# An attention and state-space kernel: the state-space half computed by another route

## The chip, the cores and the metric

The kernel runs on one core of a Trainium2 chip. The metric is the device time of one execution in microseconds (us); six runs of the kernel before are shown. The engines are TensorE (PE; PEld is its weight load), VectorE (DVE), ScalarE (ACT), GpSimd (POOL) and SyncE (SP); SP, ACT and POOL also issue DMAs, each on a queue of its own.

## The reference

Two independent results stand side by side in the output, [1, 2048, 896]: 448 columns of a linear attention, and 448 of a long convolution whose kernel K comes from a diagonal state-space model.

```python
def _A_ref(x, wqkv, w_phi, wo):            # x [1, 2048, 448], 16 heads of 28
    q, k, v = split(x @ wqkv)
    phi = lambda t: concat(softmax(t @ w_phi), softmax(-(t @ w_phi)))
    kv = einsum("bhsf,bhsd->bhfd", phi(k), v);  z = sum_s(phi(k))
    return (phi(q) @ kv / (phi(q) @ z + 1e-6)) @ wo

def _B_ref(u, A_re, A_im, B_re, B_im, C_re, C_im, log_dt, Dskip):   # u [1, 2048, 448], states 448 x 256
    dt = exp(log_dt)[:, None]
    logdA, dB = dt * (A_re + 1j * A_im), dt * (B_re + 1j * B_im)
    l = arange(2048).astype(bf16)          # rounded: only 641 different values
    K = einsum("dn,dnl,dn->dl", C, exp(logdA[:, :, None] * l), dB).real
    y = irfft(rfft(pad(u)) * rfft(pad(K)))[:2048]                   # length 4096
    return y + u * Dskip
```

The positions l are rounded to bfloat16 in the reference: 0 to 256 are exact, above that they come in steps of 2, 4 and 8.

## The kernel before

The program is written in a framework that makes the waits and orders the instructions of each engine itself, from the order of the program and from which of them it reckons to be ready. A pool that takes over the SBUF of released pools waits until these are no longer used.

`hedgehog_attention` comes first: loads of x and the weights, q, k and v (ps_qk at L195, written ahead of ps_v at L210), the exponentials and their sums, the feature sums, the result (ps_out, L423) and its stores (osb). `ssm_conv` follows in four steps.

`ssm_coefficients` loads the six parameter tables transposed (tin_Are and so on) and makes the products with dt. `ssm_build_K` makes K as a sum over states of A^(64 h) times A^l. For each half of the states (nch) and each of 8 chunks of 14 x 4 channels it doubles two tables of powers: U (UR, UI; 32 high powers times C and B) and W (WR, WI; 65 low powers), with `_cmul` (L494 to L499), six VectorE tensor_tensors a step:

```python
nc.vector.tensor_tensor(out=t1, in0=ar, in1=brb, op=ALU.mult)
nc.vector.tensor_tensor(out=t2, in0=ai, in1=bib, op=ALU.mult)
nc.vector.tensor_tensor(out=out_r, in0=t1, in1=t2, op=ALU.subtract)
...
```

For each channel two small matmuls (L609, L611) sum over 128 states: weights U of 32 columns, moved W of 65, four channels side by side in the four column groups of the array. The results go to Ts, and from there to a table kd in DRAM (L622).

`ssm_fft_conv` builds its Fourier tables on the chip, then transforms u and K in two stages each (psA at L792, then xps at L826) with a round trip through DRAM between them (SD_u, SD_k), multiplies the two spectra (L874 to L879), and transforms back in two stages with another round trip (ZD; zps, ops). The skip term u * Dskip joins in the last matmuls, and ob carries the result to the output (L936, L942).

Of the kernel before, what the change touches and what calls it, by code (L numbers as in the profile page):

```python
# [10 lines left out]
BF16 = mybir.dt.bfloat16  # L11
# [7 lines left out]
D_MODEL = 448  # L19
# [12 lines left out]


MAGIC_ROUND = 12582912.0


def round_f32(nc, out_ap, in_ap):
    nc.vector.tensor_scalar(out_ap, in_ap, MAGIC_ROUND, -MAGIC_ROUND, op0=ALU.add, op1=ALU.add)


def floor_div_const(nc, pool, out_ap, in_ap, shape, P, tag):
    t = pool.tile(shape, F32, name="fdt", tag=tag)
    nc.vector.tensor_scalar(t, in_ap, 1.0 / float(P), 0.5 / float(P) - 0.5, op0=ALU.mult, op1=ALU.add)
    round_f32(nc, out_ap, t)
# [26 lines left out]
def kernel(  # L71
# [371 lines left out]
DEBUG_TENSORS = {}  # L443
DEBUG_MODE = False
PI = float(np.pi)

N_LO = 65
N_HI = 32
N_ARG = 2 * N_LO


def ssm_coefficients(tc, B_A_re, B_A_im, B_B_re, B_B_im, B_C_re, B_C_im, B_log_dt, base_pool):
    nc = tc.nc
    A_nd = base_pool.tile([128, 2, D_MODEL], F32, name="A_nd")
    TH_nd = base_pool.tile([128, 2, D_MODEL], F32, name="TH_nd")
    CBR_nd = base_pool.tile([128, 2, D_MODEL], F32, name="CBR_nd")
    CBIN_nd = base_pool.tile([128, 2, D_MODEL], F32, name="CBIN_nd")
    with tc.tile_pool(name="coefT_in", bufs=1) as tin, \
         tc.tile_pool(name="coefT_w", bufs=1, side="right") as w:
        ldt_b = tin.tile([128, D_MODEL], BF16, name="ldt_b")  # L460
        nc.sync.dma_start(out=ldt_b[:, :], in_=bass.AP(tensor=B_log_dt.tensor, offset=B_log_dt.offset,
                                                         ap=[[0, 128], [1, D_MODEL]]))
        dt_b = tin.tile([128, D_MODEL], F32, name="dt_b32")
        nc.scalar.activation(dt_b[:, :], ldt_b[:, :], ACT.Exp)
        dtb_b = tin.tile([128, D_MODEL], BF16, name="dtb_b")
        nc.vector.tensor_copy(dtb_b[:, :], dt_b[:, :])
        for nch in range(2):
            T = {}
            for q_i, (nm, src) in enumerate((("Are", B_A_re), ("Aim", B_A_im), ("Bre", B_B_re),
                                              ("Bim", B_B_im), ("Cre", B_C_re), ("Cim", B_C_im))):  # L470
                t = tin.tile([128, D_MODEL], BF16, name=f"tin_{nm}", tag=f"tin_{nm}")
                eng = nc.sync if q_i % 2 == 0 else nc.scalar
                eng.dma_start(out=t[:, :], in_=src[:, nch * 128:(nch + 1) * 128], transpose=True)
                T[nm] = t
            nc.vector.tensor_tensor(out=A_nd[:, nch, :], in0=T["Are"][:, :], in1=dtb_b[:, :], op=ALU.mult)
            nc.vector.tensor_tensor(out=TH_nd[:, nch, :], in0=T["Aim"][:, :], in1=dtb_b[:, :], op=ALU.mult)
            dBr = w.tile([128, D_MODEL], F32, name="tdBr", tag="tdBr")
            dBi = w.tile([128, D_MODEL], F32, name="tdBi", tag="tdBi")
# [23 lines left out]
def ssm_build_K(tc, kd, A_nd, TH_nd, CBR_nd, CBIN_nd, base_pool, dbg=False):  # L502
# [4 lines left out]
    with tc.tile_pool(name="k_const", bufs=1) as cpool, \  # L507
# [6 lines left out]
        for nch in range(2):  # L514
# [26 lines left out]
            for k in (2, 4, 8, 16):  # L541
                P[k] = square(*P[k // 2], f"h{k}")
# [456 lines left out]
```

## Time and profile before

| | |
|---|---|
| median of 6 runs | 1189.57 us (1187.42 to 1190.99) |
| the profiled execution | 1189.7 us |
| its span, first to last instruction | 1187.6 us |
| TensorE / VectorE / ScalarE / GpSimd busy | 444.7 / 729.3 / 150.2 / 256.0 us |
| mean granted clock of TensorE | 0.595 of full speed |
| moved by DMA | 61.10 MB |

A busy time is the sum of an engine's instructions; shares over the whole span mix stages with different limits. PEclk is the granted clock of TensorE, 1.00 being 2.4 GHz and 0.50 being 1.2. The profile gives each instruction's start and length; instructions of one engine can overlap a little.

### The profile page before, as it was taken

The numbers are of one execution on the slowest core, as the hardware profiler recorded it, in microseconds if no ns is written. First come the engines' busy times: TensorE is split into PE (matmuls) and PEld (weight loads), VectorE is DVE, ScalarE is ACT, GpSimd is POOL, SyncE is SP. The second block draws the span as 40 slices with busy tenths as digits, with TensorE's granted clock in tenths as the row PEclk, the third lists the DMA queues.
The fourth block names the chain that finished last, engine by engine and source line by source line (L and its number), as shares of the span: only waits on it lengthen the run. The fifth ranks groups of instructions, "written<-read, shape, count | busy, mean of one in ns | idle before, by whom it ended". The sixth has DMA issues, their size and how long they took to land.

```text
span 1187.6 us, 10352 instructions
## 1 busy us (share of the span) xinstructions
PE 444.7 (37%) x3499; PEld 166.7 (14%) x3499; DVE 729.3 (61%) x1655; ACT 150.2 (13%) x200; POOL 256.0 (22%) x442
## 2 busy tenths in 40 slices
PE   1986544856800111121102112112334444163298
PEld 0221100511200111121102112110111111010021
DVE  1339337525339999999999999949423224832500
ACT  0113320001213000000000000003212222031000
POOL 1000010000008544584773753001000000010000
PEclk9995555666955565556556555555556556555555
DMA  5000000000120000000000000050575656056611
GB/s 126 1 0 1 0 0 0 4 2 0 61 52 1 1 1 1 1 1 1 1 0 2 1 1 1 2 84 10 155 213 175 148 144 248 15 130 164 248 31 31
DMA packets 60508, 61.10 MB, mean 51 GB/s; under 512 B 28904, under 2 KB 57120, under 8 KB 60224
## 3 DMA queue, kind: packets, MB, share of 16 engines
q1 hardware_dynamic: 30042, 31.22, 9.7%
q10 hardware_dynamic: 28782, 22.81, 7.1%
q0 software_dynamic: 1632, 6.42, 1.6%
q8 instruction: 27, 0.44, 0.2%
q14 instruction: 25, 0.20, 0.1%
HBM read 29.35 MB, written 27.61 MB: 48 GB/s over the span
## 4 chain that ended last, share of the span: by engine, by line
DVE 47%; PE 24%; DMA 18%; ACT 4%; issue 3%; POOL 1%; ACTq 1%; SPq 0%; DVEq 0%; POOLq 0%
DVE rt L494 5%; DVE rt L495 4%; DVE rt L498 4%; DVE rt L497 4%; PE ps_qk L195 3%; DVE WR L496 3%; DVE WI L499 3%; PE ops L930 2%; PE ops L928 2%; DMA xin<-kd 2%; PE num_ps L396 2%; DMA s2k<-SD_u 2%; PE psA L792 2%; DMA s2k<-SD_k 2%; PE ps_pq L268 2%
## 5 line engine op out<-in xcount | busy, mean ns | idle before, releaser
L609 PE MATMUL kps<-WR,UR 128*32 128x65 bf16 x896 | 64.8, 308 | 386.3 <-DVE WR L496 308.1
L609 PEld LDWEIGHTS <-UR 128*32 128x32 bf16 x896 | 49.0, 141 | 390.7 <-DVE WR L496 241.8
L792 PE MATMUL psA<-xin,FA 32*128 32x448 bf16 x128 | 51.8, 564 | 96.2 <-DVE stgA L805 34.1
L805 DVE CAST stgA<-psA 128x1792 bf16<-128x1792 f32 x16 | 32.4, 2022 | 69.1 <-PE psA L792 58.9
L611 PE MATMUL kps<-WI,UI 128*32 128x65 bf16 x896 | 60.0, 307 | 10.6 <-POOL qc32i L554 4.5
L611 PEld LDWEIGHTS <-UI 128*32 128x32 bf16 x896 | 48.1, 142 | 14.4 <-DVE WI L499 14.4
L195 PE MATMUL ps_qk<-xT,Wqkv 128*128 128x512 bf16 (+3 forms) x128 | 38.2, 411 | 28.5 <-DMA xT<-in_A_x_dram 25.6
L928 PE MATMUL ops<-ZA,IA 128*32 128x448 bf16 x64 | 35.4, 556 | 33.9 <-DMA ZA<-ZD 33.9
L499 DVE TENSOR_TENSOR WI<-rt,rt 128x448 bf16<-128x448 bf16 (+3 forms) x96 | 45.4, 473 | 0.3
L496 DVE TENSOR_TENSOR WR<-rt,rt 128x448 bf16<-128x448 bf16 (+3 forms) x96 | 44.4, 463 | 0.4
L826 PE MATMUL xps<-s2k,CB 128*32 128x448 bf16 x256 | 24.8, 484 | 46.9 <-DMA s2k<-SD_u 23.1
L905 DVE CAST Zs<-zps 128x448 bf16<-128x448 f32 x32 | 20.0, 624 | 35.0 <-PE zps L896 31.0
L554 POOL CAST qc8i<-sq_il 128x56 bf16<-128x56 f32 x16 | 38.0, 2397 | 13.7 <-DVE rt L497 12.6
L585 POOL MEMSET WR<- 128x56 bf16 x16 | 2.6, 165 | 176.5 <-PE ps_out L423 163.0
L936 DVE CAST ob<-ops 128x448 bf16<-128x448 f32 x8 | 5.0, 625 | 56.2 <-PE ops L930 56.2
L893 PE MATMUL zps<-YF,IB 32*128 32x448 bf16 x64 | 22.9, 530 | 43.2 <-DVE YF L880 24.4
L616 ACT CAST Ts<-kps 128x455 bf16<-128x455 f32 x16 | 10.2, 638 | 212.4 <-PE kps L611 212.4
L803 ACT CAST stgA<-psA 128x1792 bf16<-128x1792 f32 x16 | 26.4, 1652 | 78.1 <-PE psA L792 40.7
L341 POOL MEMSET KVBD<- 128x448 bf16 x8 | 3.4, 471 | 151.2 <-PE ps_pq L268 151.2
L930 PE MATMUL ops<-UD,IDT 32*32 32x448 bf16 x64 | 34.7, 551 | 1.4 <-DVE UD L920 1.4
L792 PEld LDWEIGHTS <-FA 32*128 32x128 bf16 x128 | 16.6, 132 | 130.5 <-issue 77.3
L554 POOL CAST pc4i<-sq_ih 128x56 bf16<-128x56 f32 x16 | 29.3, 1848 | 23.8 <-DVE rt L497 17.7
(275 smaller groups left out, 1325.6 us busy)
## 6 DMA issues: line engine op xcount, KB each, us to landing
ZA<-ZD SPq DMA_DIRECT2D x1, 7168.0 KB
SD_u<-stgA SPq DMA_DIRECT2D x8, 448.0 KB
SD_u<-stgA ACTq DMA_DIRECT2D x8, 448.0 KB
SD_k<-stgA SPq DMA_DIRECT2D x8, 448.0 KB
SD_k<-stgA ACTq DMA_DIRECT2D x8, 448.0 KB
s2k<-SD_u SPq DMA_DIRECT2D x3, 896.0 KB
s2k<-SD_u ACTq DMA_DIRECT2D x3, 896.0 KB
s2k<-SD_k SPq DMA_DIRECT2D x3, 896.0 KB
```

Source lines behind the costliest of these rows:

```text
L195: nc.tensor.matmul(ps[plo:phi, sc * 512:(sc + 1) * 512], lhsT=Wt[dci][dplo:dphi, fcol0:fcol0 + frows], rhs=xT[dci][dplo:dphi, sc * 512:(sc ...
L494: nc.vector.tensor_tensor(out=t1, in0=ar, in1=brb, op=ALU.mult)
L495: nc.vector.tensor_tensor(out=t2, in0=ai, in1=bib, op=ALU.mult)
L496: nc.vector.tensor_tensor(out=out_r, in0=t1, in1=t2, op=ALU.subtract)
L497: nc.vector.tensor_tensor(out=t1, in0=ar, in1=bib, op=ALU.mult)
L499: nc.vector.tensor_tensor(out=out_i, in0=t1, in1=t2, op=ALU.add)
L554: eng.tensor_copy(dst2d.rearrange("p (q g) -> p g q", g=4), dview(src448))
L609: nc.tensor.matmul(outap, lhsT=UR[:, :, slot], rhs=WR[:, :, slot], start=True, stop=False, tile_position=(0, 32 * g))
L611: nc.tensor.matmul(outap, lhsT=UI[:, :, slot], rhs=WI[:, :, slot], start=False, stop=True, tile_position=(0, 32 * g))
L792: nc.tensor.matmul(ps[:, n2l * 512:n2l * 512 + D_MODEL], lhsT=FA2[0:32, :], rhs=xt[0:32, 4 * j + n2l, :], start=True, stop=True,)
L928: nc.tensor.matmul(ops[32 * g2:32 * (g2 + 1), 0:D_MODEL], lhsT=IA[:, :], rhs=ZA[:, m2, :], start=True, stop=False, tile_position=(0, 32 * g2))
L930: nc.tensor.matmul(ops[32 * g2:32 * (g2 + 1), 0:D_MODEL], lhsT=IDT[0:32, :], rhs=UD[0:32, m2, :], start=False, stop=True, tile_position=(0 ...
```

## The change

Attention stays as it is, but for helper functions that stood in the file twice. `ssm_coefficients`, `ssm_build_K` and `ssm_fft_conv` go, and a new `ssm_conv` takes their place.

The Fourier tables G and F and an integer table PID (multiples p = 1, 3, 5, ... 31 of the identity) are computed when the program is built and lie in the program as constants. The six parameter tables are loaded as they lie and transposed on TensorE.

The low powers are no longer doubled. With the positions split as HI (32 values) plus LO (49 values between 0 and 128), E = exp(a l) comes from ScalarE's Exp and W = (cos, sin)(t l) from its Sin, with l as PID's odd multiple times a power of two in the operation's scale; W is then multiplied by E (`times_e`). Both halves of the states lie side by side, so E and W are made for two chunks (a quarter of the channels) at a time: 49 rows of 224 columns. U is doubled as before, with powers PW of 32 to 1024 (`hi_tables`), for one chunk of 112 columns (56 channels, two halves of the states) at a time, in two buffers. W, E and Ts have one buffer. For each channel four small matmuls of 32 columns of weights and 49 to move sum over all states, so that Ts is written once. 28 DMAs then put the 641 different values of K into rows of Kt.

The convolution is made of two blocks of 1024 and a transform of length 512 on folded halves, as dense matmuls of 128 x 128 weights with 448 columns: u's transform from UD through ab to SU (128 matmuls), K's from Kt and F to SK (112), products on VectorE (Y, S), the inverse of the first block (72 with the skip term) and of the second (64, with the skip term added by VectorE). Nothing goes through DRAM on the way.

```diff
@@ -93,8 +80,7 @@
-        ssm_conv(tc, B_u, B_A_re, B_A_im, B_B_re, B_B_im, B_C_re, B_C_im, B_log_dt, B_Dskip, out2,
-                 dbg=DEBUG_MODE)
+        ssm_conv(tc, B_u, B_A_re, B_A_im, B_B_re, B_B_im, B_C_re, B_C_im, B_log_dt, B_Dskip, out2)
@@ -440,532 +426,433 @@
-N_LO = 65
+N_LO = 49
-def ssm_coefficients(tc, B_A_re, B_A_im, B_B_re, B_B_im, B_C_re, B_C_im, B_log_dt, base_pool):
-def _cmul(nc, out_r, out_i, ar, ai, brb, bib, t1, t2, sub):
-def ssm_build_K(tc, kd, A_nd, TH_nd, CBR_nd, CBIN_nd, base_pool, dbg=False):
-def ssm_fft_conv(tc, B_u, B_Dskip, kd, out2, dbgd=None):
...
+    keep = tc.alloc_tile_pool(name="b_keep", bufs=1)
+    Kt = keep.tile([128, N_KT, D_MODEL], BF16, name="Kt")
+    SU = keep.tile([128, 2, 2, 2, 4, D_MODEL], BF16, name="SU")
+    UD = keep.tile([128, 2, 2, 4, D_MODEL], BF16, name="UD")
...
+    ps_mm = tc.alloc_tile_pool(name="b_psmm", bufs=2, space=bass.MemoryType.PSUM)
...
+        t = par.tile([112, 4, SSM_N], BF16, name=f"raw{nm}")
+        nc.sync.dma_start(out=t[:, :, :], in_=src.rearrange("(j p) n -> p j n", p=112))
...
+    for k in ("ah", "al", "th", "tl", "cr", "ci"):
+        ps = ps_mm.tile([128, 2, 512], BF16, name="ps_t", tag="mm")
...
+                nc.tensor.transpose(ps[:, nch, 112 * j:112 * j + 112], nat[k][:, j, 128 * nch:128 * nch + 128],
+                                    PID[0:112, 0, 0:112])
+            nc.scalar.copy(dst[:, :, nch * CW:(nch + 1) * CW].rearrange("p c (g q) -> p c g q", q=NQ),
+                           ps[:, nch, 0:D_MODEL].rearrange("p (g c q) -> p c g q", g=4, c=NCHK))
...
+    for k in (32, 64, 128):
+        amps[k] = pw.tile([128, NCOL], F32, name=f"amp{k}")
+        act(split(amps[k][:, :]), args["a"], ACT.Exp, scale=float(k))
+    for k in (32, 64, 128):
+        s = pw.tile([128, 2, NCOL], F32, name=f"cs{k}")
+        act(split(s[:, 0, :]), args["t"], ACT.Sin, scale=float(k), bias=bias_hp[:, :])
+        act(split(s[:, 1, :]), args["t"], ACT.Sin, scale=float(-k))
...
+    for k in (256, 512, 1024):
+        s2 = pw.tile([128, 2, NCOL], F32, name="s2", tag="s2")
+        act(s2[:, :, :], cur[:, :, :], ACT.Square)
...
+        nc.scalar.copy(PW[k][:, :, :], nxt[:, :, :])
...
+    wk = tc.alloc_tile_pool(name="b_wk", bufs=1)
+    W = wk.tile([128, 2, N_LO, 2 * COLS], BF16, name="W")
+    E = wk.tile([128, N_LO, 2 * COLS], BF16, name="E")
+    Ts = wk.tile([128, N_LO, 8 * NQ], BF16, name="Ts")
...
+                    for jt in range(4):
+                        nc.tensor.matmul(ps[:, 0:D_MODEL], lhsT=G[:, cp, jt, 128 * mt:128 * mt + 128],
+                                         rhs=ab[:, b, cp ^ st, jt, :], start=(jt == 0), stop=(jt == 3))
+                    nc.scalar.copy(SU[:, b, cp, st, mt, :], ps[:, 0:D_MODEL])
...
+    tp = tc.alloc_tile_pool(name="b_u", bufs=2, reuse_waits="tile")
...
+    def times_e(grp):
+        for r0, r1 in DONE[grp]:
+            TT(out=W[:, :, r0:r1, :], in0=W[:, :, r0:r1, :],
+               in1=E[:, r0:r1, :].unsqueeze(1).to_broadcast([128, 2, r1 - r0, 2 * COLS]), op=ALU.mult)
+
+    def table_args(src, qt, dsts, funcs, after=None):
+        q0 = qt * 2 * COLS
+        for grp in range(4):
+            ps = ps_arg.tile([128, 2, 512], F32, name="ps_a", tag="arg")
+            for e in range(4):
+                o = ps[:, e // 2, (e % 2) * 2 * COLS:(e % 2 + 1) * 2 * COLS]
+                for part in range(2):
+                    nc.tensor.matmul(o, lhsT=PID[:, 4 * grp + e, :], rhs=src[:, part, q0:q0 + 2 * COLS],
+                                     start=(part == 0), stop=(part == 1))
...
+                emit(pair(4 * grp, 4), full, 1)
+                if grp < 2:
+                    emit(pair(16 + 4 * grp, 4), full, 2)
+                    emit(pair(24 + 8 * grp, 4), full, 4)
...
+    def hi_tables(c):
+        U = tp.tile([128, N_HI, 2, COLS], BF16, name="U", tag="U")
...
+            TT(out=t1[:, 0:n], in0=src, in1=bc(0), op=ALU.mult)
+            TT(out=t2[:, 0:n], in0=src, in1=bc(1), op=ALU.mult)
+            TT(out=dst[:, :, 0, :], in0=t1[:, 0:n, 0, :], in1=t2[:, 0:n, 1, :], op=ALU.subtract)
+            TT(out=dst[:, :, 1, :], in0=t1[:, 0:n, 1, :], in1=t2[:, 0:n, 0, :], op=ALU.add)
+        step(32, U[:, 0:1], U[:, 1:2], 1)
...
+    for qt in range(4):
+        table_args(AT, qt, [E], [(ACT.Exp, 1, None)])
+        table_args(TH, qt, [W[:, 0], W[:, 1]], [(ACT.Sin, 1, bias_hp[:, :]), (ACT.Sin, 1, None)],
+                   after=times_e)
+        for c in (2 * qt, 2 * qt + 1):
+            U = hi_tables(c)
+            for hq in range(2):
+                ps = ps_kb.tile([128, 512], F32, name="ps_k", tag="kb")
+                for qq in range(7):
+                    q = 7 * hq + qq
+                    for i in range(4):
+                        nch, ri = i // 2, i % 2
+                        for g in range(4):
+                            x = nch * CW + g * NQ + q
+                            nc.tensor.matmul(ps[32 * g:32 * g + 32, qq * N_LO:(qq + 1) * N_LO],
+                                             lhsT=U[:, :, ri, x], rhs=W[:, ri, :, (c % 2) * COLS + x],
+                                             start=(i == 0), stop=(i == 3), tile_position=(0, 32 * g))
+                nc.scalar.copy(Ts[:, :, NQ * c + 7 * hq:NQ * c + 7 * hq + 7],
+                               ps[:, 0:7 * N_LO].rearrange("p (c l) -> p l c", c=7))
+    for g in range(4):
...
+                eng = nc.sync if g % 2 == 0 else nc.scalar
+                eng.dma_start(out=Kt[r:r + n, kt, cs], in_=Ts[32 * g + h0:32 * g + h1, l0:l1, :])
...
+                        terms = [(i, i) for i in range(5)] if b == 0 else [(5, 4), (6, 5)]
+                        for n, (fi, kt) in enumerate(terms):
+                            nc.tensor.matmul(ps[:, 0:D_MODEL], lhsT=ft[:, fi, 128 * mt:128 * mt + 128],
+                                             rhs=Kt[:, kt, :], start=(n == 0), stop=(n == len(terms) - 1))
+                        nc.scalar.copy(SK[:, b, cp, st, mt, :], ps[:, 0:D_MODEL])
...
+        def product(t1, t2, ub, kb, st):
+            TT(out=flat(t1[:, :, :, :]), in0=flat(SU[:, ub, :, st]), in1=bcast(SK[:, kb, 0, st]), op=ALU.mult)
+            TT(out=flat(t2[:, :, :, :]), in0=flat(SU[:, ub, :, st]), in1=bcast(SK[:, kb, 1, st]), op=ALU.mult)
...
+                    for cp in range(2):
+                        for mt in range(4):
+                            nc.tensor.matmul(ps[:, 0:D_MODEL], lhsT=G[:, cp, mt, 128 * jt:128 * jt + 128],
+                                             rhs=S[:, r, cp, mt, :], start=(b == 1 and cp == 0 and mt == 0),
+                                             stop=(cp == 1 and mt == 3))
+                    if b == 0:
+                        nc.scalar.copy(ob[:, jt, :], ps[:, 0:D_MODEL])
...
+        inverse(0)
+        for st in range(2):
...
+            product(t1, t2, 1, 0, st)
+            product(t3, t4, 0, 1, st)
...
+        inverse(1)
```

## Rows read from the trace of the kernel before

**Rows 1.** Windows by stage: us, busy of each engine, granted clock, DMA share, GB/s.

```profile
0.00:323.00 323.00, 203.59 (x1060) 63.88 (x1061) 144.53 (x226) 53.03 (x68) 8.39 (x27) 0.74 0.07 17
323.00:804.00 481.00, 67.81 (x1796) 58.92 (x1795) 434.48 (x1262) 24.57 (x35) 230.03 (x385) 0.56 0.06 10
804.00:1188.00 384.00, 173.25 (x643) 43.85 (x643) 150.28 (x168) 72.65 (x97) 17.61 (x30) 0.52 0.45 132
```

**Rows 2.** The chain that ended last, shares of the span by engine.

```profile
DVE 47%; PE 24%; DMA 18%; ACT 4%; issue 3%; POOL 1%; ACTq 1%; SPq 0%; DVEq 0%; POOLq 0%
```

**Rows 3.** The same chain in order of time: start, us, what.

```profile
27.36 6.61 PE ps_qk L195 x14
...
40.68 4.16 PE ps_v L210 x17
44.84 4.20 PE ps_qk L195 x16
...
108.45 1.77 PE ps_pk L231 x4
...
308.25 1.95 PE ps_out L423 x8
...
324.17 3.69 DMA tin_Aim<-in_B_A_im_dram
...
789.39 14.65 DMA kd<-Ts
```

**Rows 4.** Timeline of VectorE in the building of K: start, us, what.

```profile
395.63 0.38 DVE L494 TENSOR_TENSOR rt<-WR,qc8r 128x448 bf16<-128x448 bf16 x1
395.93 0.38 DVE L495 TENSOR_TENSOR rt<-WI,qc8i 128x448 bf16<-128x448 bf16 x1
...
402.04 1.09 DVE L494 TENSOR_TENSOR rt<-WR,qc32r 128x1792 bf16<-128x1792 bf16 x1
403.05 1.09 DVE L495 TENSOR_TENSOR rt<-WI,qc32i 128x1792 bf16<-128x1792 bf16 x1
```

**Rows 5.** Timeline of ScalarE in attention.

```profile
131.05 1.88 ACT L277 ACTIVATE EQ_p<-ps_pq 128x2048 bf16<-128x2048 f32 x1 [3.72 <-PE ps_pq L268]
132.83 1.87 ACT L277 ACTIVATE EQ_n<-ps_pq 128x2048 bf16<-128x2048 f32 x1
```

**Rows 6.** Groups by line: busy us, mean ns of one, idle before and its releaser.

```profile
L609 PE MATMUL kps<-WR,UR 128*32 128x65 bf16 x896 | 64.8, 308 | 386.3 <-DVE WR L496 308.1
L609 PEld LDWEIGHTS <-UR 128*32 128x32 bf16 x896 | 49.0, 141 | 390.7 <-DVE WR L496 241.8
...
L803 ACT CAST stgA<-psA 128x1792 bf16<-128x1792 f32 x16 | 26.4, 1652 | 78.1 <-PE psA L792 40.7
```

**Rows 7.** Timeline of ScalarE at the start of the SSM part: Exp L517, Sin L519.

```profile
359.77 1.28 ACT L517 ACT_TABLE_LOAD   x1
361.07 0.58 ACT L517 ACTIVATE amph<-A_nd 128x448 f32<-128x448 f32 x1
361.66 1.28 ACT L519 ACT_TABLE_LOAD   x1
362.95 0.67 ACT L519 ACTIVATE cvh<-TH_nd,bias_hp 128x448 f32<-128x448 f32 x1
```

**Rows 8.** Windows of attention after an idle stretch of TensorE, columns as in rows 1.

```profile
279.00:285.00 6.00, 5.86 (x14) 1.89 (x14) 2.67 (x4) 1.75 (x4) 0.00 (x0) 0.50 0.00 0
285.00:291.00 6.00, 6.00 (x25) 1.94 (x22) 1.77 (x3) 1.76 (x3) 0.00 (x0) 0.92 0.00 0
```

**Rows 9.** Timeline of TensorE in one run of K's small matmuls, four merged to a row.

```profile
412.39 0.36 PE L609 MATMUL kps<-WR,UR 128*32 128x65 bf16 x4
412.51 0.36 PE L611 MATMUL kps<-WI,UI 128*32 128x65 bf16 x4
412.64 0.36 PE L609 MATMUL kps<-WR,UR 128*32 128x65 bf16 x4
```

**Rows 10.** Timeline of SP's DMA issues, merged.

```profile
238.76 12.92 SPq L117 DMA_DIRECT2D zcolb<-kvdram  x30
...
910.49 14.49 SPq L862 DMA_DIRECT2D xin<-kd  x14
```

**Rows 11.** Timeline of VectorE: its last instruction.

```profile
1182.78 0.62 DVE L936 CAST ob<-ops 128x448 bf16<-128x448 f32 x1 [7.11 <-PE ops L930]
```

More of the change, by code (lines that the diff above doesn't have):

```diff
@@ L645, in sin_from_int @@
[L645 to L655 removed]
+NQ = 14
@@ L943, in ssm_fft_conv @@
[L943 to L968 removed]
+    G_np, F_np, P_np = _dft_tables()
@@ new lines, in ssm_conv @@
+    nc.sync.dma_start(out=PID[:, :, :], in_=P_d)
+    nc.sync.dma_start(out=G[:, :, :, :], in_=G_d)
+    for b in range(2):
+        for a in range(2):
+            nc.sync.dma_start(out=UD[64 * a:64 * a + 64, b, 0, :, :], in_=rep_rows(u2, 1024 * b, a, 0))
+        for t in range(4):
+            nc.gpsimd.dma_start(out=UD[:, b, 1, t, :], in_=pair_rows(u2, 1024 * b, t, 0))
+    dtb = par.tile([112, 4], BF16, name="dtb")
+    act(dtb[:, :], ldt[:, :], ACT.Exp)
+    dtf = par.tile([112, 4], F32, name="dtf")
@@ new lines, in ssm_conv @@
+    f1 = par.tile([112, 4, SSM_N], F32, name="f1")
+    f2 = par.tile([112, 4, SSM_N], F32, name="f2")
+    for dst, (x1, y1), (x2, y2), sc, op in (("cr", ("Cre", "Bre"), ("Cim", "Bim"), dtf, ALU.subtract),
+                                            ("ci", ("Cre", "Bim"), ("Cim", "Bre"), ndt, ALU.add)):
+        for f, x, y in ((f1, x1, y1), (f2, x2, y2)):
+            for j in range(4):
+                nc.vector.scalar_tensor_tensor(out=f[:, j, :], in0=raw[x][:, j, :], scalar=sc[:, j:j + 1],
+                                               in1=raw[y][:, j, :], op0=ALU.mult, op1=ALU.mult)
+        TT(out=nat[dst][:, :, :], in0=f1[:, :, :], in1=f2[:, :, :], op=op)
@@ new lines, in ssm_conv, with split @@
+    par.release()
+    pw = tc.alloc_tile_pool(name="b_pw", bufs=1)
+    ps_arg = tc.alloc_tile_pool(name="b_psarg", bufs=2, space=bass.MemoryType.PSUM)
+    ps_kb = tc.alloc_tile_pool(name="b_pskb", bufs=2, space=bass.MemoryType.PSUM)
+    NCOL = NCHK * COLS
+    def split(ap2d):
+        return ap2d.rearrange("p (a b) -> p a b", b=D_MODEL)
+    args = {}
+    for key, src in (("a", AT), ("t", TH)):
+        ps = ps_arg.tile([128, 2, 512], F32, name="ps_a", tag="arg")
+        for half in range(2):
+            for part in range(2):
+                nc.tensor.matmul(ps[:, half, 0:D_MODEL], lhsT=PID[:, 0, :],
+                                 rhs=src[:, part, half * D_MODEL:(half + 1) * D_MODEL],
+                                 start=(part == 0), stop=(part == 1))
+        args[key] = ps[:, :, 0:D_MODEL]
@@ new lines, in ssm_conv @@
+    sq = {}
+    amps = {}
+    for k in (32, 64, 128):
[5 more added lines that the diff above has]
+        act(split(s[:, 1, :]), args["t"], ACT.Sin, scale=float(-k))
+        sq[k] = s
+    for k in (32, 64, 128):
+        dst = PW[k]
+        if k == 128:
+            dst = pw.tile([128, 2, NCOL], F32, name="q128")
+        for ri in range(2):
+            TT(out=dst[:, ri, :], in0=amps[k][:, :], in1=sq[k][:, ri, :], op=ALU.mult)
@@ new lines, in ssm_conv @@
+    for g in range(4):
+        cs = slice(112 * g, 112 * g + 112)
+        for kt, h0, h1, runs in K_ROWS:
+            r = 0
+            for l0, l1 in runs:
+                n = (h1 - h0) * (l1 - l0)
+                eng = nc.sync if g % 2 == 0 else nc.scalar
+                eng.dma_start(out=Kt[r:r + n, kt, cs], in_=Ts[32 * g + h0:32 * g + h1, l0:l1, :])
+                r += n
+        eng = nc.sync if g % 2 == 0 else nc.scalar
+        eng.dma_start(out=Kt[0:1, 5, cs], in_=Ts[32 * g + 31:32 * g + 32, 48, :])
```

725 lines of the change are left out of this document (230 added, 495 removed).

## The prediction

> **What bounds the kernel now.** I read the windows by stage first [rows 1]: attention to 323 us, the building of the convolution kernel K from 323 to 804, the FFT convolution from 804 to 1188. In the middle one VectorE is busy 434 of 481 us; it makes the power tables UR, UI, WR, WI, and all else hides behind it. In the last no engine is busy half the time; its chain steps between TensorE, copies out of PSUM and round trips through DRAM. The chain of waits says the same: VectorE 47% of the span, TensorE 24%, DMA 18% [rows 2]. Its pieces in order of time show one more thing: ps_v, which stands in the program after every ps_qk, runs at 40.68, before the ps_qk of 44.84 [rows 3]. So an engine's order is not that of the program: work that is ready is moved ahead of work that waits. The whole forecast turns on this.
>
> **What goes and what stays.** Attention is untouched, and the new pools lie on its SBUF, so the SSM part can begin no earlier than its first loads do now, 324.2 [rows 3]. Everything behind, 863 us, is replaced. I count the new part from that point, S.
>
> **Prices.** VectorE, bf16 tensor_tensor: 448 elements start 0.30 us after the last one, 1792 take 1.01 [rows 4], so 0.067 us + 0.53 ns an element. ScalarE from PSUM: 2048 elements 1.78 us from start to start and 1.87 alone [rows 5]; 1792 alone 1.652 [rows 6], so 0.84 ns an element plus 0.07 us (behind another) to 0.16 (alone). A change between Exp and Sin costs one load: it starts at 359.77, the next operation at 361.07, so 1.30 us [rows 7]. TensorE, 128x128 weights and 448 columns: eight ps_out in 1.95 us, 0.244 each; four ps_pk in 1.77, 0.44 each [rows 3]. The second is the lower clock: after the idle stretch before 279 the granted clock stays 0.50 for 6 us with 14 matmuls, then 25 run in the next 6 at 0.92 [rows 8]. The small matmuls of K (32 columns of weights, 65 to move): 0.31 us each, but four column groups side by side start every 0.125 us [rows 9], so 31 ns each.
>
> **Start-up.** ScalarE carries most of it: 12 copies of transposes (0.44 each, 5.3 us), 9 Exp and Sin of 896 (7.4), 7 copies and squares of 1792 (11), 32 copies of u's transform (14.2), the first quarter's tables (33, below) and three table loads (3.9): 75 us. It starts near S+13, behind the raw parameters and the identity: 1.9 MB, 15 us at the 124 GB/s of kd<-Ts (1.82 MB in 14.65 us [rows 3]), the first of them usable before the last. VectorE's products and squarings alternate with it, and u's transform fills the gaps: 128 matmuls, 31 us at 0.244 or 57 at 0.44, begun when u and G, 2.8 MB more, are in (S+38 at that rate, S+25 at twice it, since their pieces are larger; an estimate, and I take S+25); I take S+70 for its end. With 7 us of waits the first tables E and W are done at S+95, W multiplied by E at S+97. U of the first chunk reuses the SBUF of u's input and so starts at S+70; two chunks of U and the products with E fill VectorE to S+108 (below). So the first matmuls of K run S+97 to 104, and the second chunk's S+108 to 115.
>
> **One quarter of K** (four of them). ScalarE: each table has 49 rows less one, 48 x 224 = 10752 elements in 19 pieces, 9.0 + 1.4 = 10.4 us; Exp, Cos, Sin make 31.2, the bias operand of Cos 1.9 more (estimate, 0.67 against 0.58 for 448 elements with and without one [rows 7]), two loads 2.6, four copies of K 2: 38 us. VectorE: the products W times E are 21504 elements in 11 pieces, 12 us; U is 20832 elements in 28 pieces, 13 us a chunk, two chunks 26: 38 us, against 434/4, 109, for a quarter now. TensorE: 448 small matmuls x 31 ns = 14 us, and 64 argument matmuls of 224 columns, which lie beside ScalarE. These don't simply overlap. W has one buffer, so the next Sin and Cos can be written only when both chunks' matmuls have read it; E may be made ahead, since its rows come free with the products, and U too, in two buffers. The ring is then: matmuls of two chunks 14, Cos and Sin 22.7, one load 1.3, handovers between TensorE and ScalarE 1.5, last products with E 2.2, copies in between 1.3: 43 us, with VectorE's 38 inside it. Three more rings: K is complete at S+115+129 = S+244, that is 568.
>
> **Tail.** K's 641 rows move from Ts to Kt in 28 DMAs, 14 to a queue. Issue costs from 0.43 us (30 tiny ones in 12.92) to 1.03 (14 row gathers in 14.49) [rows 10], so 6 to 14.5 us, plus some 2 to land; the bytes are no bound, since 0.57 MB in 2564 pieces is under a third of kd<-Ts, 8320 pieces in 14.65 us [rows 3]. I take 11: 580. K's transform is 112 matmuls: 13 at the lower clock in the first 6 us, 99 at 0.244, 30 us: 610 (its tables load beforehand, and the 32 copies of 0.44 hide). VectorE then multiplies: the rest of the first block's product 5.9 and half of the sums 2, so the first inverse starts at 618; its 72 matmuls take 20.5, to 639. VectorE meanwhile has 2 us of sums, some 6 left of the other half's product terms and 15.6 of this half's, 2 of sums: 643. So the second inverse waits for VectorE; 64 matmuls, again 13 of them slow, 18.5: 662. The last evacuation and its store: now it starts at 1182.78 [rows 11] and the span ends at 1187.6 (table above), 4.8 us: 667. The profiled execution took 1189.7 with a span of 1187.6, so 2.1 lie around the span: 669, against a median of 1189.6.
>
> **The other bound.** The same sum with each instruction's own length in place of the distance between starts (0.16 for ScalarE: start-up 10, ring 4 each), 8 more for u's transform at the lower clock, 5.5 for the slow issue, 0.44 for all large matmuls of the tail (K's transform +20, second inverse +10) gives 735. The matmuls of the tail are dense and the row shows the clock rising in such a stretch, so I take a third of the way: 690. For a gain or loss below these I allow 20 us: ScalarE's table groups of 224 elements are cheaper or dearer than the line through larger ones.
>
> From the end of one Exp (361.65) to the start of a Sin behind it (362.95) the trace shows 1.30 us, the load alone [rows 7]. The Trainium skill ("ScalarE: Activation LUTs", What ACT_TABLE_LOAD costs) puts such a switch at about 2.66 us, the load and a drain of 1.38 behind it. By the page the nine switches of the new part would cost 12 us more, 702; the trace does not bear it out, and the sum stays with the row.
>
> **Rivals.**
> Nothing is moved ahead: E, Sin, products, U and matmuls follow as they are written. Then a quarter is 40 of tables and tails, 26 of U, 7 of matmuls, 73 us; four after S+70 end at S+362, 118 later: about 810 (840 by full lengths). Against it stands ps_v in [rows 3]; for it, that E, W and U share two PSUM argument buffers and in-order engines, so one wrong order is enough for part of it, 740 to 780.
>
> Table loads multiply: the order chosen mixes groups of Exp of the next quarter with Sin of this one. [rows 7] shows exactly that now, Exp and Sin in turn with a load each. Eight groups a quarter are at most 8 loads for 2: 24 x 1.30 = 31 us, 720. W's single buffer speaks against it.
>
> Slower than now: the matmuls of K no longer run side by side. Their operands are read with a step of 224 elements where it is 56 now, and groups of four are built in another order. Alone, one costs 308 ns and its weights 141 [rows 6]; 1792 x (449 - 31) ns is 749 us more, 1440. It decides from 0.31 us a matmul, (1190 - 690)/1792 + 0.031. The step now already skips over most of the line, and the four column groups stay, so this is unlikely.
>
> Quicker: copies, loads and tables hide better than taken and the ring falls to VectorE's 38: 640.
>
> **How the numbers follow.** Forecast as summed, 645 to 735: 0.63. Loads multiplied, 705 to 750: 0.12. Partly or wholly in written order, 740 to 840: 0.17 (half of it under 785). Quicker than 645: 0.06. Matmuls one by one: 0.02. The likeliest time is 690. The range is 642 to 790: it leaves out the quicker tail, the wholly serial case and the slow one. Faster, same and slower by over 0.2% (2.4 us, about what a measurement of this kernel tells from no change): 0.97, 0.01, 0.02; only the matmul case, or a mishap of its size, reaches 1187.
>
> **What would show it.** Attention unchanged to 324. First matmul of K near 421. Between two quarters W's Cos and Sin begin when the matmuls of the second chunk end, 43 us after the last time; the windows of K show VectorE and ScalarE each some 85% busy. Exp of the next quarter stands on ScalarE before the last matmuls of this one; if it stands behind, the serial rival holds. Nine to eleven table loads in the whole SSM part; thirty or more would be the second rival. Small matmuls start four in 0.125 us or less. K's transform, near 580 to 610, at a granted clock of 1.00 after some 6 us; if it stays 0.50, add 20 to 30. I am wrong if ring or start-up hides a wait that I have not named: a PSUM buffer, the DMAs to Kt, or VectorE held by an order that puts products with E in front of U.

## Result, and the profile after the change

The changed kernel takes 666.6 us (median of 8 runs, 665.9 to 668.4); the one before 1189.2 (16 runs). The ratio is 0.561 [0.5603, 0.5616]. That lies in the range of 642 to 790 and within 3 us of the sum that the prediction had worked out (669), before it went "a third of the way" towards its other bound, to 690. The profiled execution of the changed kernel took 667.5 us, with a span of 665.7.

Windows by stage of the changed kernel, columns as in [rows 1]: attention; start-up of the SSM part up to the first tables; the four quarters of K; the tail.

```profile
core 0: us, PE busy (x) PEld busy (x) DVE busy (x) ACT busy (x) POOL busy (x), PEclk, DMA share, GB/s
0.00:324.00 324.00, 201.70 (x1064) 63.93 (x1064) 144.90 (x228) 53.56 (x69) 8.38 (x27) 0.74 0.07 18
324.00:425.00 101.00, 50.09 (x268) 27.93 (x268) 57.09 (x94) 77.41 (x123) 8.43 (x13) 0.73 0.23 50
425.00:571.00 146.00, 71.98 (x1969) 61.63 (x1968) 134.16 (x236) 111.23 (x192) 0.00 (x0) 0.74 0.04 14
571.00:666.00 95.00, 54.75 (x248) 25.61 (x248) 60.46 (x48) 20.03 (x41) 7.02 (x9) 0.77 0.20 47
```

Attention is as it was. K, from its first parameter to its last column, takes 247 us (324 to 571) where it took 481 in [rows 1], and the convolution 95 where it took 384; u's transform, which lay in the 384, now lies in the 247. In the third row VectorE is busy 134 of 146 us; the next view, windows inside that stretch, leaves its edges out.

```profile
440.00:480.00 40.00, 17.13 (x480) 14.86 (x477) 39.16 (x68) 35.04 (x62) 0.00 (x0) 0.74 0.01 2
480.00:520.00 40.00, 21.32 (x512) 17.51 (x511) 38.90 (x68) 34.73 (x62) 0.00 (x0) 0.71 0.01 2
520.00:560.00 40.00, 16.85 (x488) 14.68 (x488) 39.17 (x67) 29.39 (x48) 0.00 (x0) 0.70 0.01 2
```

VectorE is busy 97 to 98%, not some 85 as forecast. ScalarE's timeline in the same stretch shows the rings: each quarter has a load for Sin, with which the new cosines and sines of W begin, and one for Exp.

```profile
445.31 1.28 ACT L682 ACT_TABLE_LOAD   x1 [2.23 <-PE ps_k L742]
...
469.25 1.28 ACT L682 ACT_TABLE_LOAD   x1
...
486.57 0.45 ACT L745 CAST Ts<-ps_k 128x343 bf16<-128x343 f32 x1 [2.00 <-PE ps_k L742]
...
488.08 1.28 ACT L682 ACT_TABLE_LOAD   x1
...
528.97 1.28 ACT L682 ACT_TABLE_LOAD   x1
```

The first of these rows is the Sin load of the second quarter, the last two are those of the third and fourth; that of the first quarter starts at 399.91. From Sin to Sin: 45.4, 42.8 and 40.9 us, against a forecast of 43. The Exp load (469.25) stands ahead of the last copy of this quarter's K (486.57): the next E is made ahead, as the forecast needed. Nine loads in all, none interleaved.

### The profile page after: what moved, and what is told of

Its sections match the earlier page's. It is cut to its first block, busy times and chain, and to the rows that moved or that the text cites. A ratio compares the mean times of both kernels' runs of the same rounds, so it can differ in the third digit from the quotient of the medians.

```text
span 665.7 us, 8629 instructions
## 1 busy us (share of the span) xinstructions
PE 378.5 (57%) x3544; PEld 179.1 (27%) x3544; DVE 396.6 (60%) x604; ACT 262.2 (39%) x423; POOL 23.8 (4%) x49
## 4 chain that ended last, share of the span: by engine, by line
DVE 33%; PE 30%; ACT 13%; issue 9%; DMA 9%; ACTq 3%; POOL 1%; SPq 0%; POOLq 0%; DVEq 0%
DVE W L666 7%; PE ps_qk L181 5%; DVE t L715 4%; PE num_ps L382 3%; DVE t L716 3%; PE ps_s L786 3%; PE ps_k L742 3%; PE ps_pq L254 3%; DMA xT<-in_A_x_dram 3%; ACT W L682 3%; DVE zk L228 2%; DVE U L717 2%; PE zps L270 2%; ACT E L682 2%; DVE rZp L279 2%
## 5 line engine op out<-in xcount | busy, mean ns | idle before, releaser
L676 PEld LDWEIGHTS <-PID 128*128 128x128 bf16 x256 | 30.1, 119 | 94.5 <-issue 88.5
L682 ACT ACTIVATE W<-ps_a,bias_hp 128x896 bf16<-128x896 f32 (+2 forms) x76 | 51.3, 823 | 0.4
L742 PE MATMUL ps_k<-W,U 128*32 128x49 bf16 x1792 | 43.8, 268 | 13.3 <-DVE U L717 4.9
L666 DVE TENSOR_TENSOR W<-W,E 128x1792 bf16<-128x1792 bf16 (+2 forms) x44 | 49.3, 1171 | 0.4 <-ACT W L682 0.3
L682 ACT ACTIVATE E<-ps_a 128x896 bf16<-128x896 f32 (+2 forms) x76 | 45.2, 703 | 1.1 <-PE ps_a L676 0.9
L742 PEld LDWEIGHTS <-U 128*32 128x32 bf16 x1792 | 40.7, 138 | 17.3 <-issue 10.2
L682 ACT ACTIVATE W<-ps_a 128x896 bf16<-128x896 f32 (+2 forms) x76 | 44.8, 820 | 0.0
L827 PE MATMUL ps_o<-SD,G 128*128 128x448 bf16 x128 | 28.8, 387 | 19.9 <-DVE SD L814 19.9
L715 DVE TENSOR_TENSOR t<-U,PW 128x896 bf16<-128x896 bf16 (+3 forms) x56 | 37.8, 675 | 1.8
L716 DVE TENSOR_TENSOR t<-U,PW 128x896 bf16<-128x896 bf16 (+3 forms) x56 | 37.5, 669 | 0.0
L649 PE MATMUL ps_u<-ab,G 128*128 128x448 bf16 x128 | 31.8, 395 | 9.1 <-ACT SU L651 8.9
L717 DVE TENSOR_TENSOR U<-t,t 128x448 bf16<-128x448 bf16 (+3 forms) x56 | 23.3, 416 | 1.6
```

The source lines that it names most:

```text
L649: nc.tensor.matmul(ps[:, 0:D_MODEL], lhsT=G[:, cp, jt, 128 * mt:128 * mt + 128], rhs=ab[:, b, cp ^ st, jt, :], start=(jt == 0), stop=(jt = ...
L666: TT(out=W[:, :, r0:r1, :], in0=W[:, :, r0:r1, :], in1=E[:, r0:r1, :].unsqueeze(1).to_broadcast([128, 2, r1 - r0, 2 * COLS]), op=ALU.mult)
L676: nc.tensor.matmul(o, lhsT=PID[:, 4 * grp + e, :], rhs=src[:, part, q0:q0 + 2 * COLS], start=(part == 0), stop=(part == 1))
L682: act(out_ap, in_ap, fn, scale=float(sgn * s), **kw)
L715: TT(out=t1[:, 0:n], in0=src, in1=bc(0), op=ALU.mult)
L716: TT(out=t2[:, 0:n], in0=src, in1=bc(1), op=ALU.mult)
```

## Experiments

Runs 1 to 4 and 8 were timed once each, and are set against the kernel before on the same chip. In the first four that was 1185.7 us, also timed once; at 0.561 of it the changed kernel would take 665.2 there. The eight times of the changed kernel lie 2.5 us apart, so differences of 2 us between single runs show nothing by themselves.

**1. The written order.** In the loop over the quarters each instruction is tied behind the one that the program writes before it on its engine.

```
+    last = {}
+    for ins in list(nc.cur_bb.bb.instructions)[first:]:
+        eng = str(ins.engine)
+        if eng in last:
+            tc.add_manual_dep(ins, last[eng], ...)
+        last[eng] = ins.name
```

> Only the order changes: in the loop over the quarters of K each engine runs its instructions as the program writes them, so nothing of the next quarter is moved ahead. Theory of the prediction (work moved ahead carries the ring): a quarter becomes E 10.4 + 1.3 for its load, Cos and Sin 24 + 1.3, handovers 2, last product 2.2, U of the two chunks 28, matmuls of the second chunk 6: about 75 us where 43 stand now. Four quarters from the end of u's transform near 399: K complete near 700 instead of 571, the whole about 765 to 800 us. Rival (the order hardly matters, because VectorE alone has some 42 us of work in every quarter and everything else hides behind it in any order): 667 to 690 us.

778.1 us, 113 more. The chain of causes is in the profile: the window of a quarter (its Sin loads start at 473.84, 547.03 and 619.95), and below it VectorE's products of a quarter, in the groups by line (busy us, mean ns, idle before and its releaser).

```profile
474.00:547.00 73.00, 21.58 (x513) 18.08 (x512) 40.75 (x69) 37.02 (x63) 0.00 (x0) 0.59 0.00 1
```

```profile
L666 DVE TENSOR_TENSOR W<-W,E 128x1792 bf16<-128x1792 bf16 (+2 forms) x11 | 12.4, 1173 | 31.5 <-ACT W L682 31.4
```

The same work (VectorE 40.8, ScalarE 37 a quarter) needs 73 us, because the engines take turns: VectorE sits 31.5 us in front of the products while ScalarE makes E and W. The prediction's first rival put such a quarter at 73 and K 118 us later. So moving work ahead is worth 113 us here; the theory holds and the rival of this run (667 to 690) falls.

**2 to 4. Which ring sets the 43 us?** The prediction counted a ring through W's one buffer (43) with VectorE (38) inside it. VectorE at 97% says otherwise. Two edits, alone and together: no new cosines of W in the quarters 2 to 4 (shortens the ring through W and ScalarE's work), and no products of W with E (shortens VectorE's work).

```
-        table_args(TH, qt, [W[:, 0], W[:, 1]], [(ACT.Sin, 1, bias_hp[:, :]), (ACT.Sin, 1, None)],
-                   after=times_e)
+        table_args(TH, qt, [W[:, 1], W[:, 0]][:2 if qt == 0 else 1],
+                   [(ACT.Sin, 1, None), (ACT.Sin, 1, bias_hp[:, :])], after=times_e)
```

That is run 2; run 3 has `after=None` in the old lines, run 4 in the new ones.

> In the quarters 2, 3 and 4 one of the two tables of W (the cosine) is not made anew; the old rows are multiplied on, so the values are not those of the reference. ScalarE loses some 12 us in each of three quarters, VectorE and TensorE keep all their work. Theory A (VectorE's work, now 42 us a quarter, sets the pace): no more than 4 us less, 662 to 667 us. Theory B (the ring through W's one buffer sets it, as the prediction summed it: matmuls, cosine and sine, load, handovers, last products): up to 3 x 11 = 33 us less, stopped only by VectorE; with VectorE at the 38 us that the prediction gave it, 3 x 5 = 15 us less, about 651. Theory C (both are within 2 us of each other): 3 to 6 us less, and much more only in the kernel that takes both away.

> The products of W with E on VectorE are left out, so K lacks its exponential factor. VectorE loses 12.3 us a quarter (49.3 us in all), ScalarE and TensorE keep all their work. Theory A (VectorE sets the pace): 37 to 49 us less, 618 to 630 us. Theory B (the ring through W sets it): only the last products, 2.2 us a quarter, leave the ring: 657 to 660 us. Theory C (both nearly equal): 3 to 4 us a quarter less, 650 to 660 us, until the ring through W or ScalarE's own 40 us stop it.

> Both of the last two together: no products of W with E, and no new cosine table in the quarters 2 to 4. VectorE has some 30 us a quarter left (two chunks of U), ScalarE some 28, the ring through W some 28. Theory A: the same as without the products alone, 618 to 630 us. Theory B: the same as without the cosine plus the last products, about 645 us or, if VectorE was no limit at all, 625. Theory C (two limits nearly equal): about 12 us a quarter less, 615 to 625 us, while each alone gave less than a third of that.

Measured: 664.6, 663.3 and 630.2 us: 0.6, 1.9 and 35 less than 665.2. From the first Sin load to the fourth it is 126.9, 128.0 and 103.0 us, where the changed kernel has 129.1. A window of the run without the new cosines, then of the one without the products, then of the one without both (columns as above):

```profile
440.00:480.00 40.00, 20.35 (x484) 17.27 (x480) 39.22 (x67) 25.55 (x44) 0.00 (x0) 0.67 0.01 1
```

```profile
440.00:480.00 40.00, 20.07 (x505) 16.79 (x503) 24.81 (x53) 34.16 (x60) 0.00 (x0) 0.72 0.01 2
```

```profile
444.00:475.00 31.00, 20.33 (x514) 17.13 (x512) 28.50 (x59) 25.45 (x45) 0.00 (x0) 0.83 0.01 2
```

With the first edit ScalarE falls from 35 to 25 of 40 us and next to nothing is won: VectorE stays at 39, and K's matmuls of the second chunk wait 5.6 us for its U.

```profile
479.39 5.31 PE L742 MATMUL ps_k<-W,U 128*32 128x49 bf16 x224 [5.62 <-DVE U L717]
```

Its quarters are 40.8 and 41.1 us long, so VectorE's work sets a limit of 41 us. With the second VectorE falls to 25 and again next to nothing is won: it now waits for U's buffers, which K's matmuls hold, as the waits of that run show (total, times, longest):

```profile
DVE U L706 <- PE ps_k L742: 27.6, 3, 13.5
```

The Sin loads of that run are 42.8, 43.1 and 42.1 us apart. The length is the one that the prediction summed for the ring through W, but the pieces are not. TensorE's and ScalarE's rows of that run, at the end of a quarter:

```profile
477.06 0.72 PE L742 MATMUL ps_k<-W,U 128*32 128x49 bf16 x21 [0.93 <-issue]
478.75 4.15 ACT L682 ACTIVATE E<-ps_a 128x896 bf16<-128x896 f32 x5 [0.49 <-PE ps_a L676]
484.74 1.28 ACT L682 ACT_TABLE_LOAD   x1 [0.56 <-PE ps_a L676]
```

K's matmuls have read W by 477.8, and the Sin load starts only at 484.7: in between ScalarE makes the last six pieces of the next E, whose arguments stand behind K's matmuls on TensorE. The prediction had all of E outside the ring. With both edits the quarters are 30.8 us long, and VectorE is busy 28.5 of 31.

So theory A (VectorE alone; it wanted 37 to 49 us from the second edit) and theory B (the ring through W alone; at least 15 from the first) both fall. C holds in this sense: behind VectorE's 41 us stands a second limit of 42 to 43, which is felt as soon as VectorE is relieved. Its sizes were missed: it wanted 3 to 6 us from the first edit, a time of 650 to 660 us with the second and 615 to 625 with both. As the order on TensorE and ScalarE is another one in run 3, that run does not show how long the ring through W is in the changed kernel; the rows under "The ring" below do.

**5. The early U.** In the changed kernel VectorE waits 23 us, because U of the first chunk reuses the SBUF of `ab`, u's transform's input. The waits of the changed kernel from 375 to 600:

```profile
DVE UD L774 <- DMA DSK<-in_B_Dskip_dram: 26.9, 1, 26.9
DVE U L706 <- PE ps_u L649: 23.0, 1, 23.0
```

```
+    below_ab, ab = [fwd.tile([128, 2, 2, 4, D_MODEL], BF16, name=n) for n in ("below_ab", "ab")]
...
+        with tc.issue_after(U0_end) if c == 1 else ExitStack():
             nc.vector.tensor_copy(U[:, 0, :, :], CBc[:, c, :, :])
...
+    U0 = hi_tables(0)
+    U0_end = nc.cur_bb.bb.instructions[-1]
+    U1 = hi_tables(1)
```

Both tables of the first quarter are traced before the loop; the products with E are issued behind the copy with which U1 begins.

> The table U of the first chunk gets SBUF of its own, below the input of u's transform, and stands on VectorE ahead of everything of K, so that it can run from 377 us, where VectorE sits idle for 23 us in the changed kernel because U of the first chunk reuses that input's SBUF. No work is added or taken away. Theory C (VectorE and the ring through W both need about 43 us a quarter): both chunks of the first quarter are ready when W is, the first quarter ends 6 to 9 us earlier (the next Sin's load at 437 to 439 instead of 445), and then the ring through W keeps its 43: 657 to 661 us. If VectorE alone set the pace, the whole table, 14.7 us, comes off: about 652. If the idle time costs nothing: 666.

667.9 us, ratio 0.5627 [0.5614, 0.5639]: no gain, but 0.0017 more, some 2 us; the intervals just overlap. Its waits and TensorE's timeline tell where the 14.5 us went:

```profile
DVE W L667 <- ACT W L683: 9.8, 1, 9.8
DVE U L708 <- PE ps_u L649: 8.7, 1, 8.7
DVE U L708 <- PE ps_k L751: 6.8, 1, 6.8
```

```profile
429.06 1.65 PE L677 MATMUL ps_a<-AT,PID 128*128 128x224 bf16 x8 [5.07 <-ACT E L683]
432.30 1.65 PE L677 MATMUL ps_a<-AT,PID 128*128 128x224 bf16 x8 [1.59 <-ACT E L683]
...
434.44 9.41 PE L751 MATMUL ps_k<-W,U 128*32 128x49 bf16 x401
```

The 23 us became 9.8 + 8.7 + 6.8 = 25.3: the wait moved. W was complete at 429 instead of 425, since U's steps now stood between the products; and TensorE had the arguments of the next quarter's E queued ahead of K's first matmuls, which so began at 434.4 instead of 425.0. The Sin load of the second quarter came at 446.1 (445.3 before), 47.3 us behind that of the first where it was 45.4.

**6. Kt through three queues.** The 24 large DMAs from Ts to Kt go round SP, ScalarE and GpSimd.

```
-                eng = nc.sync if g % 2 == 0 else nc.scalar
+                eng = (nc.sync, nc.scalar, nc.gpsimd)[n_dma[0] % 3]; n_dma[0] += 1
```

> The 28 DMAs from Ts to Kt go to three queues (10, 10 and 8, GpSimd's the third) instead of two of 14. The prediction's 11 us for this step were 14 to 17. If the issue, now 0.94 us a DMA, one behind the other, sets it: four fewer on each queue, 3.8 us less, 662 to 664 us. If the landing or the engines of the DMA set it, or GpSimd issues more slowly than the others (its one DMA so far took 3.3 us from issue to landing): no change or up to 5 us more, 666 to 672.

661.3 us, ratio 0.5574 [0.5566, 0.5583], 4.2 us less by the ratios. ScalarE's issues after the last copy of K, first in the changed kernel, then in this one, and GpSimd's:

```profile
571.31 5.74 ACTq L754 DMA_DIRECT2D Kt<-Ts  x6
...
583.13 0.58 ACTq L757 DMA_DIRECT2D Kt<-Ts  x1
```

```profile
567.33 3.46 ACTq L755 DMA_DIRECT2D Kt<-Ts  x4
...
575.12 0.76 ACTq L758 DMA_DIRECT2D Kt<-Ts  x1
```

```profile
567.60 4.63 POOL L755 DMA_DIRECT2D Kt<-Ts  x8 [192.94 <-ACT Ts L745]
```

Issuing takes 8.6 us instead of 12.4; GpSimd is not slower: an issue of these 24 takes it 0.61 us in the median, SP 0.63 and ScalarE 0.77. From the start of the last copy of K to the start of the last matmul of K's transform it is 33.5 us instead of 35.8, so 2.3 of the 4.2 are shown to be this step's. The profiled execution also left attention 2 us earlier, which is no work of this edit; where the rest of the 4.2 comes from is open.

**7. Both together.**

> Both of the last two together. They lie in stretches that follow each other, so their gains add: 653 to 658 us, if each does what it should (7 and 4 us); the sum of the two measured differences in any case.

665.1 us, ratio 0.5603 [0.5594, 0.5612]: 0.0024 below the early U alone, 2.9 us, which agrees with the 2.3 of the profile. The expected 653 to 658 was missed, as the early U brought nothing; that the two differences add (2 more and 4.2 less) holds within the intervals.

**8. What a table change costs.** The kernel of run 1, with Exp in the place of Sin for W.

```
-                   [(ACT.Sin, 1, bias_hp[:, :]), (ACT.Sin, 1, None)]
+                   [(ACT.Exp, 1, bias_hp[:, :]), (ACT.Exp, 1, None)]
```

> The kernel that keeps the written order (778.1 us), with the cosines and sines of W's tables made as Exp, so that ScalarE changes no table in the loop; the values of W are not those of the reference. In the written order ScalarE's tables lie bare on the path (no other engine works beside them), so each table change costs its whole price. Eight loads in the loop, of which the first, before the first E, stays or moves, so seven fewer: by the row of the trace, 1.30 us each, 9 us less: 768 to 770 us. By the page of the Trainium skill, 2.66 each with the drain behind the load: 19 us less, 758 to 760 us. If Exp and Sin differ in their own length, the rows of both tell it.

769.7 us beside 1186.7 for the kernel before, 769.1 scaled to the chip of run 1: 9.0 less, for seven loads 1.29 us each; single runs leave some 0.3 us of doubt on each, and 2.66 would have needed 19 us. The tables themselves are unchanged: a cosine piece takes 821 ns in the mean in both kernels, a sine piece 818 and 819. A quarter is 70.6 us from first copy of K to first copy of K (440.60 to 511.19), 2.4 less than the 73 of run 1, with two loads fewer.

**9. The early U, mended.** U of the second chunk stands whole ahead of the first products, and two groups of arguments stand behind the first chunk's matmuls; Kt goes through three queues.

```
+                  with tc.issue_after(K0_end[0]) if src is AT and qt == 1 and grp > 1 else ExitStack():
                     nc.tensor.matmul(o, lhsT=PID[:, 4 * grp + e, :], ...
```

> The kernel with the early table U and three queues for Kt, once more, with the order mended in two places: U of the second chunk stands whole ahead of the first products of W with E on VectorE, and on TensorE the last two groups of arguments for the next quarter's E stand behind the first chunk's matmuls of K. Before, both had pushed the first matmuls of K from 425 to 434 us and given back what the early U brought. If that explains the missing gain, K's first matmuls start near 426, the Sin load of the second quarter comes at 440 to 442 instead of 446, and after that the ring through W keeps its 43 us: 655 to 659 us. If the early U brings nothing for another reason (the ring through W, once VectorE is ahead, runs slower than 43): 661, as with the three queues alone.

657.4 us, ratio 0.5534 [0.5508, 0.556], 4.8 us below run 6 by the ratios (interval 2 to 8), and 8 below run 7, which does the same work in another order. TensorE's timeline, and VectorE's waits from 375 to 600:

```profile
424.36 5.32 PE L750 MATMUL ps_k<-W,U 128*32 128x49 bf16 x224 [0.18 <-DVE W L667]
432.82 5.39 PE L750 MATMUL ps_k<-W,U 128*32 128x49 bf16 x224 [3.15 <-ACT Ts L755]
```

```profile
DVE U L709 <- PE ps_u L649: 8.7, 1, 8.7
DVE U L709 <- PE ps_k L750: 7.8, 3, 5.4
DVE t L811 <- ACT SK L799: 1.5, 1, 1.5
```

K begins at 424.4 and the second quarter's Sin load is at 441.1, inside the expected 440 to 442. Of VectorE's 23.0 us of idle time 16.5 are still there (the first two rows), since the second chunk's U still waits for u's transform, and the third's and fourth's for buffers that K's matmuls hold; 6.5 are used, of which some 5 show in the time. The next quarters take 39.5 and 40.9 us, and VectorE is busy 38.3 and 39.9 of them.

**10. D applied early.** The other long wait of VectorE (26.9 us, above) is for D, loaded after K because its SBUF is free only then; four products of 4.1 us in all then stand at the head of the tail.

```
+    DSK = keep.tile([128, D_MODEL], BF16, name="DSK")
...
+    with tc.issue_after(U0_end):
+        for b in range(2):
+            for r in range(2):
+                TT(out=UD[:, b, r, :, :], in0=UD[:, b, r, :, :],
+                   in1=DSK[:, :].unsqueeze(1).to_broadcast([128, 4, D_MODEL]), op=ALU.mult)
```

> The last kernel, and the multiplication of u by D taken out of the tail: D is loaded in the start-up instead of after K, and VectorE does the four products (4.1 us) in its idle time before u's transform ends, not at the head of the tail. If VectorE bounds the tail, as its gapless row from 589 to 645 us in the changed kernel says, these 4 us come off: 652 to 655 us. If the tail waits for the copies SK out of PSUM and the products would only start later, 1 us or nothing: 656 to 658.

657.5 us, ratio 0.5528 [0.5508, 0.5548]: 0.7 us less by the ratios, with an interval from 5 less to 3 more, so the times alone do not exclude the 4 us. VectorE's timeline in the tail of this kernel tells more:

```profile
582.49 3.96 DVE L811 TENSOR_TENSOR t<-SU,SK 128x3584 bf16<-128x3584 bf16 x2 [25.45 <-ACT SK L800]
587.73 3.96 DVE L812 TENSOR_TENSOR t<-SU,SK 128x3584 bf16<-128x3584 bf16 x2 [1.28 <-ACT SK L800]
...
598.33 2.03 DVE L812 TENSOR_TENSOR t<-SU,SK 128x3584 bf16<-128x3584 bf16 x1 [2.50 <-ACT SK L800]
```

The four products had been done while K's transform was still on its way; without them VectorE waits for the copies SK instead. From the last copy of K to the first sums behind the products (SD) it is 37.4 us, and 36.7 in run 9. In run 9 VectorE had already waited 1.5 us for SK in this place (the third row of its waits above), so the four products were not on the path: a second tie, and a miss of the expectation, which had read nearly unbroken work as a limit.

## Why the prediction was right, and where it was not

**The start.** W multiplied by E was forecast for S+97 and was complete at 424.9, S+101; u's transform for S+70, and its last copy started at 398.5, S+74. Four us too early, in a sum of 75 us of ScalarE work; ScalarE is busy 77.4 of 101 us there. The first quarter ended 6 us late (Sin load at 445.3, where the sum had S+115), and the rest of K took 125.5 us where it had 129; so K's end, 3 us off, is two errors that cancel in part.

**Work moved ahead.** The whole forecast turned on this, read from one ps_v in [rows 3]. It was right, and run 1 gives it a price: 73 us a quarter without, 43 with, 113 us in all. The chance of 0.17 for that rival was for a real danger, and its sum (118 us later) was nearly exact. One of its grounds was misread: U needs no PSUM argument buffer, only E and W share the two.

**The ring.** Its number (43) was met, with 42.8 and 40.9 in the middle quarters, but not by its terms: the step "with VectorE's 38 inside it" was wrong. TensorE's rows of the third quarter, between the Sin loads of 488.08 and 528.97:

```profile
513.51 5.35 PE L742 MATMUL ps_k<-W,U 128*32 128x49 bf16 x224 [0.19 <-DVE W L666]
...
521.46 5.66 PE L742 MATMUL ps_k<-W,U 128*32 128x49 bf16 x224 [1.72 <-DVE U L717]
```

Load, cosines and sines take 23.5 us, the last products 1.9, the matmuls 5.4 and 5.7 (14 in the sum), the handover at the end 1.8: 38.3. The other 2.6 lie between the two runs of matmuls, where those of the second chunk wait for VectorE's U. So the ring through W has 38 us where the sum had 43, and VectorE, with 41, sets the pace where the sum had 38 for it (the one wait of VectorE that its timeline shows from 424 to 562 is 0.3 us): the two had changed places, and that 43 came out is largely luck. Products of the 1792 form start 1.0 us apart as in [rows 4], but a chunk of U takes 14.5 us, not 13. VectorE's timeline shows why:

```profile
487.95 1.09 DVE L715 TENSOR_TENSOR t<-U,PW 128x1792 bf16<-128x1792 bf16 x1
488.96 1.08 DVE L716 TENSOR_TENSOR t<-U,PW 128x1792 bf16<-128x1792 bf16 x1
490.08 0.63 DVE L717 TENSOR_TENSOR U<-t,t 128x896 bf16<-128x896 bf16 x1
490.62 0.62 DVE L718 TENSOR_TENSOR U<-t,t 128x896 bf16<-128x896 bf16 x1
491.27 0.62 DVE L715 TENSOR_TENSOR t<-U,PW 128x896 bf16<-128x896 bf16 x1
...
553.14 1.09 DVE L666 TENSOR_TENSOR W<-W,E 128x1792 bf16<-128x1792 bf16 x1
554.14 0.62 DVE L717 TENSOR_TENSOR U<-t,t 128x896 bf16<-128x896 bf16 x1
```

After an independent instruction the next starts at 1.01 or 0.54 us, after one whose result it reads at 1.12 or 0.65. The last two rows are the check: with a product of another table in between, the same subtraction (L717) starts after 1.00, so it is the dependence and not the change of operation or size that costs 0.11. Two of the four instructions of each step wait so, 14 a chunk, 1.5 us. So the "quicker" rival, a ring of 38 us and 640 in all, was not there to be had: VectorE's own work is 41, and runs 2 and 3 show that taking work from one side alone wins 2 us at most.

**Small matmuls.** Forecast 31 ns each; the row that follows gives 5.14/216 = 24, so the rival in which they run one by one, which was to decide from 310 ns, fell by more than a factor of ten.

```profile
481.38 5.14 PE L742 MATMUL ps_k<-W,U 128*32 128x49 bf16 x216
```

**Table loads.** Nine, as forecast, in place of the rival's thirty. By the page of the Trainium skill ("ScalarE: Activation LUTs", What ACT_TABLE_LOAD costs) a switch costs about 2.66 us with the drain behind the load; run 8 gives 1.29 for the whole switch, so the row was the one to sum with.

**The tail.** K was forecast complete at 568, and the last copy starts at 570.8. Then the terms erred both ways. TensorE's timeline and the granted clock (windows, columns as above):

```profile
584.94 15.24 PE L786 MATMUL ps_s<-Kt,ft 128*128 128x448 bf16 x70 [0.23 <-DMA Kt<-Ts]
...
611.38 7.90 PE L827 MATMUL ps_o<-SD,G 128*128 128x448 bf16 x32 [3.19 <-DVE SD L814]
...
642.79 14.20 PE L827 MATMUL ps_o<-SD,G 128*128 128x448 bf16 x64 [16.71 <-DVE SD L814]
```

```profile
580.00:590.00 10.00, 7.77 (x24) 2.82 (x25) 0.62 (x1) 1.97 (x4) 0.58 (x1) 0.56 0.23 38
590.00:600.00 10.00, 10.00 (x54) 5.18 (x53) 10.00 (x8) 7.37 (x16) 0.00 (x0) 1.00 0.55 176
```

The way to Kt (11 us) took 14 until the matmuls ran without gaps, since a queue issues its 14 DMAs in 12.4 us. K's transform (30) took 22 from there: it runs at 0.56 at first and at 1.00 from 590 on, as forecast, but its matmuls then start some 0.19 us apart (54 in 10 us), not 0.244. VectorE's work from the end of the transform to the second inverse (33) took 36, from 606.6 to 642.8. The second inverse waits for VectorE as the sum said, and its start (forecast 643, begun 642.8) agrees so well only because these errors cancel. It takes 14.2 us, not 18.5; the end behind it takes 8.7 (from the start of the last evacuation, 657.0, to the end of the span), not 4.8. The net of the whole sum is 2 us.

**The last step.** From 669 the forecast went to 690, "a third of the way" to a bound with full lengths and the lower clock. No row asked for it: the bound's terms were alternatives to rows that had been read (starts, not lengths, are what follow each other; the clock rose in the dense stretch of [rows 8], and did so here, from 0.56 to 1.00). That is the step that failed, by 21 us, and it is nearly the whole miss of 23.

## What to carry to other kernels

Sum a ring engine by engine from the distances between starts, dependent pairs priced apart, and keep that sum: bounds belong into the range, not into the middle. Where two rings come out within a few us, expect nothing from shortening one; a pair of edits, alone and together, shows the tie in three runs, and the trace of each then has to say what its limit is made of, since an edit can change the order as well as the work. An idle stretch is worth filling only if what follows was waiting for that very work: ask which buffer and which queue position come next, since both early-U kernels did the same work and only the order on TensorE and VectorE made one of them pay.

## What the runs showed of the hardware that was not expected

A VectorE instruction that reads the result of the one just before it started 0.11 us later than an independent one (1.12 against 1.01 us, 0.65 against 0.54), and with one independent instruction in between it did not (1.00). Small matmuls in four column groups, with operands read at a step of 224 elements, started every 24 ns. GpSimd issued the DMAs to Kt in 0.59 to 0.63 us each (run 6), where SP and ScalarE took 0.6 to 1.2 in the same stretch. The last store took 7.4 us from the start of GpSimd's issue (658.3) to the end of the span.
